# The second GEMM of a spectral mixer: two narrow products become one wide one

## The chip, the cores and the metric

The kernel runs on one core of a Trainium2 chip. The metric is the device time of one execution in microseconds; the lower, the better. The kernel before took 381.93 us, the median of three executions (381.85 to 384.48).

The engines are called as in the profile: PE (matrix products; PEld is its weight load), DVE (vector), ACT (activation), POOL and SP. Here POOL and SP mostly issue transfers in the part of the kernel that is changed.

## The reference

The input is one sequence of S = 2048 tokens with D = 512 channels. Two branches read its normalised form: a 2-D Fourier filter, and a token-mixing MLP with F = 1792 hidden units. The output joins them.

```python
def _B_ref(x, w1, b1, w2, b2):
    h = _layernorm(x, axis=-1)                      # (B, S, D)
    u = jnp.einsum("bsd,sf->bdf", h, w1) + b1       # (B, D, F)
    u = _gelu(u)
    y = jnp.einsum("bdf,fs->bds", u, w2) + b2       # (B, D, S)
    return y.transpose(0, 2, 1)

x = A_x
xn = _layernorm(x, axis=-1)
s = _A_ref(xn, A_w_r, A_w_i)      # irfft2(rfft2(xn) * (w_r + 1j w_i))
g = _silu(_B_ref(xn, B_w1, B_b1, B_w2, B_b2))
return x + s * g
```

All inputs and the output are float32.

## The kernel before

The program has two large parts. The first (up to about 204.7 us) computes the normalisation, the first GEMM (u = gelu(w1 h + b1)) and the forward Fourier transform with its filter. The second, which the change is about, computes the second GEMM, the inverse transform, the gate and the output.

**Precision.** PE is fed with a reduced float32 type. Each float32 operand is split into a high part (a copy by ACT, rounded to that type) and a low part (the difference, by DVE). A product of two operands is then three matmuls: high by high, high by low, low by high. This is the inner loop over `a` at line 940.

**Blocks.** The tokens are laid out as 16 blocks j of 128. The second GEMM works on pairs: pair p takes block j0 = p and block j1 = p + 8, for p = 0 to 7. With the halves of F and the halves of the channels this is a product of 2 x 2 blocks, and it is computed with seven block products instead of eight (a Strassen-like scheme). Each block product is called a form, numbered 1 to 7 and run in the order 1, 2, 5, 6, 3, 7, 4 (`ORDER`). Each form sums over seven tiles of 128 hidden units (`FORMS`), so it is 7 x 3 = 21 matmuls. The operand of w2 for form n is a tile w2f (high part at index 0, low part at index 1), built from loaded blocks a11, a12, a21, s4 and the running sum s1. The operand of u is a tile of 512 columns: 256 high, 256 low (tiles fa, fb, fc, fd; `form_parts` cuts them in two). Those were made once, the last of them (tiles 5 and 6) in the first microseconds of this part.

**PSUM.** Eight banks of 512 float32 columns. In the second GEMM a form uses the first 256 columns of a bank: bx (bank 2 or 3, by the parity of p), by (bank 4), bz (bank 5). Forms 6, 7 and 4 go on summing in the bank of form 1, form 3 in that of form 5. Between them ACT copies a partial sum out: p1 after form 1, v2 after form 6, p5 after form 5 (`copied`, lines 894 to 897). The four output blocks of the pair are c11 = by + p1, c12 = bz + v2, c22 = bx + p5 (DVE adds, `summed`), and c21, which is bx itself after form 4. ACT gates each with a sigmoid-weighted unit (`gate`), DVE multiplies by the filtered branch (`finish`), and a transfer that POOL issues adds it to the output in memory.

**Inverse transform.** Between the forms PE also does four blocks of eight small instructions per pair: `sequence` (line 866) and `channels` (line 875), one of each for j0 and j1. `sequence` writes bank 0 or bank 1, `channels` bank 6 or 7. ACT copies the first's result to a tile yt, which `channels` reads.

**Order.** The engines run their queues in order. In the first part and in the first microseconds of the second, the order is written out by hand (the string `STEPS` and the calls of `rest`, `forms`, `wforms` in lines 815 to 841, with `strict` set). After that the framework's scheduler places the instructions, except those that `keep` holds in program order. `ready` holds w2f tiles made ahead; the pool has three buffers. SP's queue issues the loads of w2 and the gathers yj of the transform's input, in order; POOL's issues the transfers that add the second block to s1 and s4.

**The hand-over (pair 0).** Forms of u for tiles 5 and 6 are still being made when form 1 of pair 0 starts. The sources u of these forms lie in memory (`lstage`) that the last pool `fp` takes over when they are done. The tile p1_0 of the kernel before is allocated in `fp`.

The two lines that cost the matmuls of this part:

```python
for a, (wi, ui) in enumerate(((0, uh), (0, ul), (1, uh))):
    in_turn(j0, T.matmul(o, wf[:, wi, i], ui, start=m + a == 0 and n in (1, 2, 5), stop=m == NH - 1 and a == 2,
```

Of the kernel before, what the change touches and what calls it, by code (L numbers as in the profile page):

```python
# [8 lines left out]
F32 = mybir.dt.float32  # L9
# [109 lines left out]
def spectral_mixer_kernel(tc, x, w1, b1, w2, b2, wk, we, wx, c_f, c_ft, c_d, c_i, c_g, c_h, c_s, out):  # L119
# [11 lines left out]
    def pool(stack, side, name, bufs):  # L131
        return stack.enter_context(tc.tile_pool(name=name, bufs=bufs, side=side, reuse_waits="tile"))
# [9 lines left out]
    with tc.tile_pool(name="ps", bufs=1, space=PSUM) as psp, ExitStack() as left, ExitStack() as right:  # L142
# [222 lines left out]

        def form_parts(n, i):
            t, k = form[i][n]
            return t[:, k, :D // 2], t[:, k, D // 2:]

# [384 lines left out]
        V, A, G, SY = free  # L754
        w2p = pool(right, "right", "w2", 3)
        NP, HD = NJ // 2, D // 2
        ORDER = (1, 2, 5, 6, 3, 7, 4)
# [25 lines left out]
        def w2_forms():  # L783

            for p in range(NP):
                yield w2_form(f"1_{p}", cur["a12"])
                yield w2_form(f"2_{p}", cur["a11"])
                w = w2_form(f"5_{p}", cur["s1"])
                ordered(V.tensor_add(cur["s1"], cur["s1"], cur["a12"]))
                yield w  # L790
                w = w2_form(f"6_{p}", cur["s1"])
                if p == 0:
                    yield w
                if p + 1 < NP:
                    nxt["s1"] = s1_load(p + 1, (w2p, fp)[(p + 1) % 2])
                    nxt["a12"] = w2_load("a12", w2p, p + 1, 1)
                if p:
                    yield w
                V.tensor_add(cur["s1"], cur["s1"], cur["a11"])  # L799
                w = w2_form(f"3_{p}", cur["s1"])  # L800
                if p + 1 < NP:
                    nxt["a11"] = w2_load("a11", w2p, p + 1, 0)
                yield w
                w = w2_form(f"7_{p}", cur["s4"])
                if p + 1 < NP:
                    nxt["s4"] = w2_load("s4", w2p, p + 1, 1, (p + 1 + NP, 1))
                yield w
                w = w2_form(f"4_{p}", cur["a21"])
                if p + 1 < NP:
                    nxt["a21"] = w2_load("a21", fp, p + 1 + NP, 0)  # L810
                    cur.update(nxt)
                yield w
# [4 lines left out]
        strict.append(True)  # L817
        ready = [next(wforms) for _ in range(3)]

        def rest(units, *gelus):  # L820
            for _ in range(units):
                next(streams["h"])
            for _ in gelus:
                next(streams["g"])
        rest(SPLIT, 5)
        rest(4, 12)
        last, last6 = forms(5), forms(6)
        next(last)
        next(last)
        rest(4, 13)  # L830
# [3 lines left out]
        next(last6)  # L834
        next(last6)
        next(last)
        next(last6)
        ready.append(next(wforms))
        run(last)
        run(last6)  # L840
# [3 lines left out]
        HW = [P, HD]  # L844
        made = {"p1_0": fp.tile(HW, F32, name="p1_0", tag="p1")}
        gs = [fp.tile([P, D], F32, name=f"g{j}", tag="g", bufs=3) for j in (0, NP)]
# [16 lines left out]
        def sequence(j, yj):  # L863
            pf = ps[:, j // NP].rearrange("p (b c) -> p b c", c=P)
            for b in range(4):
                in_turn(j, T.matmul(pf[:, b], yj[:, b * P:(b + 1) * P], cft, start=True, stop=True))  # L866
            yt = fp.tile([P, 4, P], F32, name=f"yt{j}", tag="yt", bufs=2)
            A.activation(yt, pf, AF.Copy)
            return yt
# [24 lines left out]
        def copied(name, src):  # L894
            t = made.pop(name, None) or fp.tile([P, HD], F32, name=name, tag=name.split("_")[0])
            A.activation(t, src, AF.Copy)  # L896
            return t

        def gate(g, j, cols, src, scale):
            A.activation(g[:, cols], src, AF.Silu, bias=b2t[:, j:j + 1], scale=scale)  # L900

        def summed(name, a, b):
            t = made.pop(name, None) or fp.tile([P, HD], F32, name=name, tag="c", bufs=2)
            V.tensor_add(t, a, b)  # L904
            return t
# [14 lines left out]
        for p in range(NP):  # L920
# [3 lines left out]
            if p == NP - 1:  # L924
                xr = fp.tile([P, D], F32, name="xr", tag="yj", bufs=3)
                SY.dma_start(xr, x[:, NJ - 1])
            bx, by, bz = ps[:, 2 + p % 2, :HD], ps[:, 4, :HD], ps[:, 5, :HD]
            for k, n in enumerate(ORDER):
# [6 lines left out]
                if k == 5 and p + 1 < NP:  # L935
                    yd = gathered(j1 + 1)
                o = {1: bx, 6: bx, 7: bx, 4: bx, 2: by, 5: bz, 3: bz}[n]
                for m, i in enumerate(FORMS):
                    uh, ul = form_parts(n, i)
                    for a, (wi, ui) in enumerate(((0, uh), (0, ul), (1, uh))):  # L940
                        in_turn(j0, T.matmul(o, wf[:, wi, i], ui, start=m + a == 0 and n in (1, 2, 5), stop=m == NH - 1 and a == 2,  # L941
                                             skip_group_check=n in (6, 3, 7, 4)))
                if n == 1:
# [20 lines left out]
                elif n == 7:  # L964
                    gate(g1, j1, right_, summed(f"c22_{p}", bx, p5), -1.0)
                    if p == 0:
# [6 lines left out]
                else:  # L973
                    gate(g1, j1, left_, bx, -1.0)
                    finish(g1, j1, whole if p + 1 < NP else left_, y1, xr)
# [40 lines left out]
```

## Time and profile before

| | |
|---|---|
| Median of three executions | 381.93 us (381.85 to 384.48) |
| The profiled execution | 382.29 us, of which its span (first to last instruction) is 380.5 us |
| Granted clock of PE | 1.00 throughout |
| Matmuls of the second GEMM, line 941 | 1176 of 256 columns |
| Period of a middle pair | 21.06 us |
| Start of form 1 of pair 0 | 204.70 us |

The profile gives times in us from the start of the span. A row of the groups by line reads: line, engine, operation, output<-input, shapes and count | busy us, mean ns of one | idle time just before, and who ended it. A row of the timeline reads: start, length, engine, line, operation. The length of a matmul or a DVE instruction is longer than its distance to the next one, since they are pipelined; where a rate is needed, the distance of the starts, or the chain of waits, is the better source. L941 is line 941 of the kernel before; lines of the changed kernel are some 1 to 22 higher.

### The profile page before, as it was taken

How to read it: one execution, taken by the hardware profiler on the slowest of the kernel's cores; microseconds unless marked ns; L12 is line 12 of the kernel's file. 1: busy time of each engine (PE TensorE's matmuls, PEld its weight loads, DVE VectorE, ACT ScalarE, POOL GpSimd, SP SyncE). 2: the span in 40 equal slices, each digit the busy share in tenths (PEclk: the TensorE clock that was granted, in tenths of full speed). 3: DMA queues.
4: the chain of work that ended last, by engine and by line, in shares of the span. 5: the costliest groups of instructions: out<-in, count | busy, mean ns of one | idle time of the engine just before them, and what ended most of it. 6: DMA issues, size and time to landing. Idle time of an engine off the chain costs nothing.

```text
span 380.5 us, 7482 instructions
## 1 busy us (share of the span) xinstructions
PE 369.8 (97%) x2760; PEld 327.8 (86%) x2760; DVE 309.0 (81%) x660; ACT 213.3 (56%) x384; POOL 102.3 (27%) x133
## 2 busy tenths in 40 slices
PE   8999999999999999999999799999999999999994
PEld 4888888888877676777779799999999999999994
DVE  5899999865799999999967798776767768777763
ACT  4677755754972365865456765545555555545541
POOL 2133233243511735765400011020303020200100
PEclk9999999999999999999999999999999999999999
DMA  7956467214455767999866599898888888895602
GB/s 249 323 190 231 133 222 239 91 42 128 120 196 179 253 213 258 283 280 307 194 181 155 149 267 188 265 164 263 168 246 184 223 204 193 194 217 158 100 0 56
DMA packets 41945, 73.32 MB, mean 193 GB/s; under 512 B 4180, under 2 KB 25172, under 8 KB 41780
## 3 DMA queue, kind: packets, MB, share of 16 engines
q1 hardware_dynamic: 35460, 58.88, 48.6%
q0 software_dynamic: 6448, 13.96, 21.4%
q8 instruction: 21, 0.34, 0.4%
q14 instruction: 16, 0.13, 0.1%
HBM read 60.24 MB, written 8.13 MB: 180 GB/s over the span
## 4 chain that ended last, share of the span: by engine, by line
PE 86%; DVE 8%; issue 2%; ACT 2%; DMA 1%; SPq 0%; DVEq 0%; ACTq 0%
PE ps L941 34%; PE ps L395 19%; PE ps L678 6%; PE ps L679 5%; PE ps L226 4%; PE ps L687 4%; PE ps L866 4%; PE ps L586 4%; PE ps L875 4%; DVE pq L128 2%; DVE e L128 2%; PE ps L665 1%; PE ps L681 1%; PE ps L600 1%; DMA x<-in_x_dram 1%
## 5 line engine op out<-in xcount | busy, mean ns | idle before, releaser
L395 PE MATMUL ps<-h,w1h 128*128 128x512 f32 x224 | 58.5, 398 | 0.0
L395 PEld LDWEIGHTS ps<-h,w1h 128*128 128x128 f32 x224 | 40.8, 188 | 8.1 <-ACT w1h L387 0.2
L776 DVE TENSOR_TENSOR w2f<-s,w2f 128x896 fp32r<-128x896 f32 x32 | 35.0, 1092 | 14.8 <-ACT w2f L775 13.7
L766 POOL DMA_DIRECT2D s<-in_w_dram x16 | 13.8, 865 | 122.7 <-DMA s<-in_w_dram 35.0
L678 PE MATMUL ps<-h,w1h 128*128 128x512 f32 x112 | 44.9, 401 | 0.0
L679 PE MATMUL ps<-h,w1h 128*128 128x512 f32 x112 | 43.7, 390 | 0.0
L941 PE MATMUL ps<-fb,w2f 128*128 128x256 f32 x336 | 42.9, 282 | 0.6 <-DVE c L904 0.6
L941 PE MATMUL ps<-fa,w2f 128*128 128x256 f32 x336 | 43.4, 283 | 0.0
L941 PE MATMUL ps<-fc,w2f 128*128 128x256 f32 x336 | 41.1, 279 | 2.1 <-ACT p L896 2.1
L941 PEld LDWEIGHTS ps<-fc,w2f 128*128 128x128 f32 x336 | 40.1, 188 | 2.3 <-ACT p L896 2.3
L941 PEld LDWEIGHTS ps<-fb,w2f 128*128 128x128 f32 x336 | 40.6, 188 | 1.4 <-issue 0.8
L941 PEld LDWEIGHTS ps<-fa,w2f 128*128 128x128 f32 x336 | 40.6, 188 | 0.0
L775 ACT ACTIVATE w2f<-s 128x896 fp32r<-128x896 f32 x32 | 30.3, 948 | 16.5 <-DVE s L799 13.5
L776 DVE TENSOR_TENSOR w2f<-a,w2f 128x896 fp32r<-128x896 f32 x24 | 26.1, 1089 | 15.8 <-ACT w2f L775 15.7
L128 POOL TENSOR_TENSOR s<-z,e 128x4 f32<-128x4 f32 x8 | 25.3, 3163 | 37.4 <-DMA z<-e 16.6
L775 ACT ACTIVATE w2f<-a 128x896 fp32r<-128x896 f32 x24 | 22.8, 950 | 21.7 <-PE ps L941 18.2
L395 PE MATMUL ps<-h,w1l 128*128 128x512 f32 x112 | 30.7, 390 | 0.1
L128 ACT ACTIVATE w1h<-w1s 128x512 fp32r<-128x512 f32 (+1 forms) x30 | 17.4, 581 | 22.2 <-PE ps L679 12.9
L678 PEld LDWEIGHTS ps<-h,w1h 128*128 128x128 f32 x112 | 21.0, 188 | 9.0 <-issue 5.0
L687 PE MATMUL ps<-h,w1l 128*128 128x512 f32 x93 | 25.6, 391 | 0.1
L395 PEld LDWEIGHTS ps<-h,w1l 128*128 128x128 f32 x112 | 20.9, 188 | 5.0 <-DVE w1l L390 0.5
L679 PEld LDWEIGHTS ps<-h,w1h 128*128 128x128 f32 x112 | 21.1, 188 | 4.0
(132 smaller groups left out, 730.8 us busy)
## 6 DMA issues: line engine op xcount, KB each, us to landing
a<-in_w_dram SPq DMA_DIRECT2D x24, 448.0 KB
s<-in_w_dram POOLq DMA_DIRECT2D x17, 448.0 KB, 7.0
s<-in_w_dram SPq DMA_DIRECT2D x15, 448.0 KB
w1r<-in_w_dram SPq DMA_DIRECT2D x16, 256.0 KB
z<-e SPq DMA_DIRECT2D x16, 256.0 KB
w1s<-in_w_dram SPq DMA_DIRECT2D x16, 256.0 KB
yj<-ey SPq DMA_DIRECT2D x16, 256.0 KB
x<-in_x_dram SPq DMA_DIRECT2D x15, 256.0 KB
```

Of the source, the lines that this page charges most:

```text
L128: return lambda *a, **k: keep(getattr(engine, name)(*a, **k))
L226: T.matmul(z[:, b], h[:, b * P:(b + 1) * P], c, start=True, stop=True)
L395: T.matmul(ps[:, bank + i], w[wi][:, i * P:(i + 1) * P], hj, start=first and j == 0, stop=last and j == NJ - 1)
L586: keep(T.matmul(pd[:, b * P:(b + 1) * P], ey[:, lo, b].rearrange("p h j -> p (h j)"), cd[:, b], start=True, stop=True))
L678: keep(T.matmul(o, wh[:, sl], hh[j], start=first, stop=False))
L679: keep(T.matmul(o, wh[:, sl], hl[j], start=False, stop=False))
L687: keep(T.matmul(ps[:, bank], wl[:, k * P:k * P + P], hh[j], start=False, stop=final))
L775: ordered(A.activation(wf[:, 0], v, AF.Copy))
L776: ordered(V.tensor_sub(wf[:, 1], v, wf[:, 0].bitcast(F32)))
L866: in_turn(j, T.matmul(pf[:, b], yj[:, b * P:(b + 1) * P], cft, start=True, stop=True))
L875: in_turn(j, T.matmul(pe[:, b % 2, b // 2], yt[:, b], ci[:, b], start=True, stop=True))
L941: in_turn(j0, T.matmul(o, wf[:, wi, i], ui, start=m + a == 0 and n in (1, 2, 5), stop=m == NH - 1 and a == 2, skip_group_check=n in (6, 3, ...
```

## The change

For the pairs 0 to 6 (`both`), the two matmuls with the high part of w2 become one over the whole tile of u, 512 columns, into the whole bank: the high-by-high sums stand in the bank's left half, the high-by-low sums in its right half. The matmul with the low part of w2 adds its 256 columns to the right half. Where a partial sum is read, the right half is now added by one more DVE instruction (`copied`, `summed`). Form 4 gets bank 1 (bw) to itself instead of summing in bx; what bx holds after form 7 is copied out (x22) and goes into c22 and c21. `sequence` uses bank 0 for both blocks. The last pair keeps three matmuls of 256 columns and its banks as before. p1_0 is allocated in the pool of w2's tiles. In the hand-over, w2's form 5 is made after a gelu of tile 5 instead of before, the s1 add later, and the forms of u for tiles 5 and 6 interleave in another order.

```diff
-        def form_parts(n, i):
+        def form_whole(n, i):
             t, k = form[i][n]
-            return t[:, k, :D // 2], t[:, k, D // 2:]
+            return t[:, k]
...
         w2p = pool(right, "right", "w2", 3)
+        p1_0 = w2p.tile([P, D // 2], F32, name="p1_0", tag="p1", bufs=1)
...
-                w = w2_form(f"5_{p}", cur["s1"])
+                yield w2_form(f"5_{p}", cur["s1"])
                 ordered(V.tensor_add(cur["s1"], cur["s1"], cur["a12"]))
-                yield w
+                if p == 0:
+                    yield
...
-        ready = [next(wforms) for _ in range(3)]
+        ready = [next(wforms) for _ in range(2)]
...
         rest(SPLIT, 5)
+        ready.append(next(wforms))
         rest(4, 12)
         last, last6 = forms(5), forms(6)
-        next(last)
-        next(last)
+        for _ in range(3):
+            next(last)
         rest(4, 13)
         rest(4, 6)
         next(last6)
         next(last)
         next(last6)
-        next(last6)
-        next(last)
+        next(wforms)
         next(last6)
         ready.append(next(wforms))
+        next(last6)
         run(last)
         run(last6)
...
-        made = {"p1_0": fp.tile(HW, F32, name="p1_0", tag="p1")}
+        made = {"p1_0": p1_0}
...
-            pf = ps[:, j // NP].rearrange("p (b c) -> p b c", c=P)
+            pf = ps[:, 0].rearrange("p (b c) -> p b c", c=P)
...
         def copied(name, src):
-            t = made.pop(name, None) or fp.tile([P, HD], F32, name=name, tag=name.split("_")[0])
-            A.activation(t, src, AF.Copy)
+            tag = name.split("_")[0]
+            t = made.pop(name, None) or (fp, w2p)[tag == "p1"].tile([P, HD], F32, name=name, tag=tag, bufs=1)
+            A.activation(t, src[:, :HD], AF.Copy)
+            if whole_bank(src):
+                V.tensor_add(t, t, src[:, HD:])
             return t
+
+        def whole_bank(src):
+            return src.shape[-1] == D
...
-            V.tensor_add(t, a, b)
+            V.tensor_add(t, a[:, :HD], b)
+            if whole_bank(a):
+                V.tensor_add(t, t, a[:, HD:])
...
-            bx, by, bz = ps[:, 2 + p % 2, :HD], ps[:, 4, :HD], ps[:, 5, :HD]
+            both = p + 1 < NP
+            bx, by, bz, bw = (ps[:, b] if both else ps[:, b, :HD] for b in (2 + p % 2, 4, 5, 1))
...
-                o = {1: bx, 6: bx, 7: bx, 4: bx, 2: by, 5: bz, 3: bz}[n]
+                o = {1: bx, 6: bx, 7: bx, 4: bw if both else bx, 2: by, 5: bz, 3: bz}[n]
+                opens, joins = n in (1, 2, 5), n in (6, 3, 7) or n == 4 and not both
                 for m, i in enumerate(FORMS):
-                    uh, ul = form_parts(n, i)
-                    for a, (wi, ui) in enumerate(((0, uh), (0, ul), (1, uh))):
-                        in_turn(j0, T.matmul(o, wf[:, wi, i], ui, start=m + a == 0 and n in (1, 2, 5), stop=m == NH - 1 and a == 2,
-                                             skip_group_check=n in (6, 3, 7, 4)))
+                    u, end = form_whole(n, i), m == NH - 1
+                    if both:
+                        in_turn(j0, T.matmul(o, wf[:, 0, i], u, start=m == 0 and not joins, stop=end,
+                                             skip_group_check=True))
+                        in_turn(j0, T.matmul(o[:, HD:], wf[:, 1, i], u[:, :HD], start=False, stop=end,
+                                             skip_group_check=True))
...
                 elif n == 7:
-                    gate(g1, j1, right_, summed(f"c22_{p}", bx, p5), -1.0)
+                    if both:
+                        x22 = copied(f"v2_{p}x", bx)
+                    gate(g1, j1, right_, summed(f"c22_{p}", x22 if both else bx, p5), -1.0)
...
-                    gate(g1, j1, left_, bx, -1.0)
+                    gate(g1, j1, left_, summed(f"c21_{p}", bw, x22) if both else bx, -1.0)
```

More of the change, by code (lines that the diff above doesn't have):

```diff
@@ L936, in spectral_mixer_kernel @@
                     yd = gathered(j1 + 1)
-                o = {1: bx, 6: bx, 7: bx, 4: bx, 2: by, 5: bz, 3: bz}[n]
+                o = {1: bx, 6: bx, 7: bx, 4: bw if both else bx, 2: by, 5: bz, 3: bz}[n]
+                opens, joins = n in (1, 2, 5), n in (6, 3, 7) or n == 4 and not both
                 for m, i in enumerate(FORMS):
-                    uh, ul = form_parts(n, i)
-                    for a, (wi, ui) in enumerate(((0, uh), (0, ul), (1, uh))):
-                        in_turn(j0, T.matmul(o, wf[:, wi, i], ui, start=m + a == 0 and n in (1, 2, 5), stop=m == NH - 1 and a == 2,
-                                             skip_group_check=n in (6, 3, 7, 4)))
+                    u, end = form_whole(n, i), m == NH - 1
[4 more added lines that the diff above has]
+                                             skip_group_check=True))
+                    else:
+                        for a, (wi, ui) in enumerate(((0, u[:, :HD]), (0, u[:, HD:]), (1, u[:, :HD]))):
+                            T.matmul(o, wf[:, wi, i], ui, start=m + a == 0 and opens, stop=end and a == 2,
+                                     skip_group_check=joins)
                 if n == 1:
```

## The prediction

> **What bounds the kernel now.** I read the busy shares first, then one middle pair of the second GEMM by engine, then the chain that ended last, then that pair in order of time.
>
> ```profile
> PE 369.8 (97%) x2760; PEld 327.8 (86%) x2760; DVE 309.0 (81%) x660; ACT 213.3 (56%) x384; POOL 102.3 (27%) x133
> 250.65:271.71 21.06, 21.06 (x183) 20.96 (x181) 15.52 (x31) 10.79 (x19) 3.51 (x4) 1.00 0.87 210
> ```
>
> The second row is the pair p=2: columns after the width 21.06 are busy PE, weight loads, DVE, ACT, POOL, then granted clock, DMA share, GB/s. PE has no free time, DVE 5.5 us, ACT 10.3 us; the clock is at 1.00.
>
> ```profile
> 21.38 4.79 PE ps L395 x21
> ...
> 161.50 0.91 PE ps L687 x4
> ...
> 240.61 0.89 PE ps L875 x8
> 241.50 4.95 PE ps L941 x42
> 246.45 0.89 PE ps L866 x8
> 247.34 2.65 PE ps L941 x21
> 249.99 0.89 PE ps L875 x8
> 250.88 2.48 PE ps L941 x21
> 253.36 0.89 PE ps L866 x8
> 254.25 7.42 PE ps L941 x63
> ...
> 352.67 2.65 PE ps L941 x21
> ```
>
> These are pieces of the chain (start, length). The eight from 240.61 are one whole pair and nothing but PE: seven forms of 21 products and four blocks of inverse transform, 21.06 us together. So the pair costs what its products cost. A product of 256 columns takes 4.95/42 = 117.9 ns; one of 512 columns, in the first GEMM, 4.79/21 = 228.1 ns (0.91/4 = 227.5 in a later stretch). The form at 247.34 (form 4) takes 2.65 instead of 2.48: 0.17 us are a wait.
>
> **Term 1, the wide product.** Per tile of w2 and form, three products of 256 columns become one of 512 and one of 256. The trace has no stream that mixes the widths, so I add the rows: 228.1 + 117.9 = 346.0 instead of 353.6 ns, 7.6 ns saved. Seven pairs (the last keeps the old form) x 7 forms x 7 tiles = 343 times: 2.6 us, all on the path. At one end the wide product saves nothing over two narrow ones (0 us); at the other it takes 227.5 (2.8 us). That it costs more than two narrow ones I exclude, since 228.1 is already less than 235.7 with the same number of columns passed. The middle row is the one with equal tile shapes and type, so 2.6.
>
> [...]
>
> **Term 2, form 4 gets its own bank.** PE around the block before form 4 in pair 3, before and after; fb are the tiles of u, w2f those of w2, yj the transform's input.
>
> ```order
> L941 MATMUL ps<-fb_2503,w2f_3_3402 128x256 x3
> L866 MATMUL ps<-cft,yj_3377 128x128 [waits DMAHW2_49]
> L866 MATMUL ps<-cft,yj_3377 128x128 x3
> L941 MATMUL ps<-fb_1432,w2f_3_3448 128x256 [waits DVE_49,Activation_49]
> L941 MATMUL ps<-fb_1432,w2f_3_3448 128x256 x2
> ```
>
> The same place on PE after the change (L955 is the wide product, L957 the narrow one):
>
> ```order
> L955 MATMUL ps<-fb_2507,w2f_3_3270 128x512
> L957 MATMUL ps<-fb_2507,w2f_3_3270 128x256
> L870 MATMUL ps<-cft,yj_3251 128x128 [waits DMAHW1_49]
> L870 MATMUL ps<-cft,yj_3251 128x128 x3
> L955 MATMUL ps<-fb_1432,w2f_3_3310 128x512 [waits Activation_49]
> L957 MATMUL ps<-fb_1432,w2f_3_3310 128x256 [waits DVE_49]
> ```
>
> The DVE wait of form 4's first product moved to the second, where it is only the low part of w2. The trace shows the old wait:
>
> ```profile
> 256.34 1.09 DVE L799 TENSOR_TENSOR s<-s,a 128x896 f32<-128x896 f32 x1
> ...
> 257.35 0.42 DVE L904 TENSOR_TENSOR c<-ps,p 128x256 f32<-128x256 f32 x1
> ...
> 258.53 1.09 DVE L776 TENSOR_TENSOR w2f<-s,w2f 128x896 fp32r<-128x896 f32 x1 [0.76 <-ACT w2f L775]
> ...
> 262.32 2.72 PE L941 MATMUL ps<-fa,w2f 128*128 128x256 f32 x21
> ...
> 267.79 0.42 DVE L904 TENSOR_TENSOR c<-ps,p 128x256 f32<-128x256 f32 x1
> ...
> 268.35 2.71 PE L941 MATMUL ps<-fb,w2f 128*128 128x256 f32 x21
> ...
> 268.86 0.58 ACT L868 ACTIVATE yt<-ps 128x512 f32<-128x512 f32 x1
> ...
> 270.90 1.05 PE L875 MATMUL ps<-cd,yt 128*128 128x128 f32 x8
> ```
>
> c22 is read out of the shared bank until 268.21, and form 4 starts at 268.35. The 2.65 recurs once in each of the pairs 1 to 6 (247.34 the first, 352.67 the last): 6 x 0.17 = 1.0 us goes, and nothing else is late at that place, since form 4's weights are made a whole form earlier. Pair 7 keeps its wait.
>
> **Term 3, what DVE and ACT get in a pair.** Bank halves have to be joined: one add more after p1, p5, v2, c11, c12, the new copy x22, and two for c21, eight adds; ACT copies x22 and in exchange gates from SBUF. Prices:
>
> ```profile
> L941 PE MATMUL ps<-fb,w2f 128*128 128x256 f32 x336 | 42.9, 282 | 0.6 <-DVE c L904 0.6
> L941 PE MATMUL ps<-fc,w2f 128*128 128x256 f32 x336 | 41.1, 279 | 2.1 <-ACT p L896 2.1
> ...
> L775 ACT ACTIVATE w2f<-s 128x896 fp32r<-128x896 f32 x32 | 30.3, 948 | 16.5 <-DVE s L799 13.5 <-DVE s L789 3.0
> ...
> L904 DVE TENSOR_TENSOR c<-ps,p 128x256 f32<-128x256 f32 x16 | 6.7, 417 | 0.0
> ...
> L896 ACT ACTIVATE p<-ps 128x256 f32<-128x256 f32 x16 | 6.1, 385 | 16.2 <-PE ps L941 14.9 <-DVE fb L296 1.4
> ```
>
> These are groups by line (busy us, mean ns of one, idle before); two DVE steps of the size of an add, in order of time:
>
> ```profile
> 273.45 0.42 DVE L879 TENSOR_TENSOR es<-ps,od 128x256 f32<-128x256 f32 x1
> 273.79 0.41 DVE L880 TENSOR_TENSOR es<-ps,od 128x256 f32<-128x256 f32 x1
> ```
>
> An add lasts 0.42 us, but the next instruction starts 0.34 us after it. So DVE gets 8 x 0.34 to 8 x 0.42 = 2.7 to 3.3 us on top of 15.5, together 18.2 to 18.8 of a pair of 20.5 us (21.06 - 49 x 0.0076 - 0.17). It fits, if no chain runs late. DVE in pair 5 around c11, before (w2fN is the split of w2 for form N, s1 the running sum of w2's blocks, p and c the copies and sums of PSUM):
>
> ```order
> L776 TENSOR_TENSOR w2f6_5_3847<-s1_13_3596,w2f6_5_3847 128x896 [waits PE_49,Activation_49]
> L799 TENSOR_TENSOR s1_13_3596<-s1_13_3596,a11_5_3629 128x896 [waits DVE_49]
> L904 TENSOR_TENSOR c11_5_3876<-ps_58,p1_5_3839 128x256 [waits PE_49]
> L776 TENSOR_TENSOR w2f3_5_3880<-s1_13_3596,w2f3_5_3880 128x896 [waits Activation_49]
> L776 TENSOR_TENSOR w2f7_5_3910<-s4_5_3659,w2f7_5_3910 128x896 [waits DMASW2_49,PE_49,Activation_49]
> ```
>
> And the same stretch of DVE after:
>
> ```order
> L903 TENSOR_TENSOR p1_5_3641<-p1_5_3641,ps_58 128x256 [waits Activation_49]
> L778 TENSOR_TENSOR w2f6_5_3651<-s1_13_3438,w2f6_5_3651 128x896 [waits Activation_49]
> L914 TENSOR_TENSOR c11_5_3673<-ps_58,p1_5_3641 128x256 [waits DVE_49,PE_49]
> L802 TENSOR_TENSOR s1_13_3438<-s1_13_3438,a11_5_3465 128x896 [waits DVE_49]
> L916 TENSOR_TENSOR c11_5_3673<-c11_5_3673,ps_58 128x256 [waits DVE_49]
> L778 TENSOR_TENSOR w2f3_5_3678<-s1_13_3438,w2f3_5_3678 128x896 [waits Activation_49]
> L903 TENSOR_TENSOR p5_5_3699<-p5_5_3699,ps_58 128x256 [waits Activation_49]
> L778 TENSOR_TENSOR w2f7_5_3702<-s4_5_3489,w2f7_5_3702 128x896 [waits DMASW2_49,Activation_49]
> ```
>
> The sum s1 now stands behind c11, so behind the end of form 2: it starts about 257.7 instead of 256.34. Queued behind it are form 3's weights, done at 259.62 today while form 3 starts at 262.32: of 2.7 us of slack 1.35 go, and p5's add, for which form 3 now waits, takes 0.4 more. About 0.95 is left. The other tight chain is ACT's before the block at 270.90: yt is done at 269.44, 1.46 us ahead; the x22 copy (0.39) and the gate of c12 (taken as long, now behind w2's copy) come before it, and 0.7 is left. So I put this term at 0; without the cover each late microsecond costs seven.
>
> **Term 4, the start (pair 0).** The 2.1 us that PE waits on "ACT p" (row above) are one wait, form 6 of pair 0.
>
> ```profile
> 203.45 0.33 SPq L764 DMA_DIRECT2D a<-in_w_dram  x1
> 203.83 1.38 SPq L853 DMA_DIRECT2D yj<-ey  x2
> 204.70 2.63 PE L941 MATMUL ps<-fd,w2f 128*128 128x256 f32 x21
> 205.93 0.42 DVE L296 TENSOR_TENSOR fd<-u,fd 128x256 fp32r<-128x256 f32 x1 [1.60 <-ACT fd L295]
> 208.70 0.42 DVE L315 TENSOR_TENSOR u<-u 128x256 f32<-128x256 f32 x1
> ...
> 210.08 0.43 DVE L318 SCALAR_TENSOR_TENSOR u<-u 128x256 f32<-128x256 f32 x1
> 210.42 1.29 DVE L296 TENSOR_TENSOR fc<-u,fc 128x512 fp32r<-128x512 f32 x2
> 212.63 1.28 DVE L296 TENSOR_TENSOR fb<-u,fb 128x512 fp32r<-128x512 f32 x2
> 213.84 1.08 DVE L799 TENSOR_TENSOR s<-s,a 128x896 f32<-128x896 f32 x1
> 214.39 2.65 PE L941 MATMUL ps<-fc,w2f 128*128 128x256 f32 x21 [2.11 <-ACT p L896]
> ```
>
> p1_0 lay in memory that fb's sources held; now it has its own tile, and the wait goes. But DVE is reordered. DVE's rows behind the u steps of tile 6, before (fa to fd are the forms of u, with the tile's number):
>
> ```order
> L296 TENSOR_TENSOR fc5_2500<-u5_2438,fc5_2500 128x2x256 [waits PE_49,Activation_49]
> L296 TENSOR_TENSOR fc6_2504<-u6_2470,fc6_2504 128x2x256 [waits PE_49,Activation_49]
> L776 TENSOR_TENSOR w2f6_0_2507<-s1_8_2406,w2f6_0_2507 128x896 [waits Activation_49]
> L296 TENSOR_TENSOR fb5_2499<-u5_2438,fb5_2499 128x2x256 [waits Activation_49]
> L296 TENSOR_TENSOR fb6_2503<-u6_2470,fb6_2503 128x2x256 [waits Activation_49]
> L799 TENSOR_TENSOR s1_8_2406<-s1_8_2406,a11_0_2411 128x896 [waits DVE_49]
> ```
>
> And DVE after, from the s1 add that stood far ahead of them:
>
> ```order
> L791 TENSOR_TENSOR s1_8_2407<-s1_8_2407,a12_0_2410 128x896
> L315 TENSOR_TENSOR u6_2474<-u6_2474 128x256 [waits DVE_49]
> L903 TENSOR_TENSOR p1_0_2406<-p1_0_2406,ps_58 128x256 [waits Activation_49]
> L316 TENSOR_TENSOR u6_2474<-u6_2474 128x256 [waits DVE_49]
> L317 SCALAR_TENSOR_TENSOR u6_2474<-u6_2474 128x256 [waits DVE_49]
> L318 SCALAR_TENSOR_TENSOR u6_2474<-u6_2474 128x256 [waits DVE_49]
> L778 TENSOR_TENSOR w2f6_0_2504<-s1_8_2407,w2f6_0_2504 128x896 [waits Activation_49]
> L296 TENSOR_TENSOR fc6_2508<-u6_2474,fc6_2508 128x2x256 [waits Activation_49]
> ```
>
> fc6's low part now comes behind the s1 add, p1's add and w2f6. From 205.93: fd 0.42, fc5 and fa6 0.65 each, s1 1.08, four u steps 1.8, p1 0.42, w2f6 1.08, fc6 0.65, less overlaps of 0.07: done at 212.3 or so. Form 5 wants it at 204.70 + 2 x 2.42 + 6/7 x 2.42 = 211.6 (2.42 is a form of seven 346 ns): a new wait of 0.75. Form 6 then starts at 212.7, 1.7 earlier, 0.15 of it term 1. Form 3's weights: s1 behind fb (1.28) and its own 1.08, done 214.7; ACT 0.95 beside three adds of DVE; low part 1.09: 216.9, while PE wants it at 212.7 + 2.42 + 0.89 + 0.23 = 216.2. So 0.65 is lost again. Net 1.7 - 0.15 - 0.65 = 0.9 us. Ends: 2.1 (no new wait) and -1.1 (rival C).
>
> **Sum.** 2.6 + 1.0 + 0 + 0.9 = 4.5 us. The profiled execution took 382.29 us, 1.8 outside its span: 377.8. It lies 0.36 above the median of 381.93, so 377.4 as a median.
>
> **Rivals.** B, the wide product saves nothing, because the fixed part of a product is set by its neighbour's weight load and not by the count: 382.3 - 1.9 = 380.4, by the median 380.0. For it: weight loads are busy 20.96 of 21.06 us; against it: wide products in a row already run at 7.6 ns less. [...]
>
> C, pair 0 loses more than it gains. The load of a12 waits for the s1 add, now done at 208.7, and the two yj gathers and a21 stand behind it on SP: they leave 5.3 us later.
>
> ```profile
> s<-in_w_dram POOLq DMA_DIRECT2D x17, 448.0 KB, 7.0
> ```
>
> If a gather takes 8 us from 209.1, the block after form 6, wanted at 215.1, waits 2.0: term 4 is -1.1 and the median 382.29 - 2.5 - 0.36 = 379.4. Against it: the queue is nearly empty then.
>
> D, slower: DVE becomes the bound at form 3.
>
> ```profile
> DVE w2f L776 <- ACT w2f L775: 29.4, 31, 3.2
> ```
>
> This row of the waits (us in total, times, longest) gives 29.4/8 = 3.7 us per pair. If each add costs 0.46 (the spacing of the four dependent DVE steps from 208.70 to 210.08) a pair is 15.5 + 3.7 = 19.2 us of DVE, and if its waits on ACT stay, since form 3's chain goes DVE, ACT, DVE, 22.9: 7 x 1.8 = 12.9 us more, 0.9 less at the start, median 394. It decides once form 3's chain is over 0.95 us later than worked out. Against it: the 0.34 us spacing.
>
> [...]
>
> **Numbers.** A measurement here can tell 1% from no change, 378.1 and 385.7. Forecast 0.60, B 0.12, C 0.15, D 0.13. Of the forecast's 0.60 I put 0.06 above 378.1, from its terms' ends: faster 0.54, same 0.33, slower 0.13. The range takes the terms' better ends, 2.8 + 1.0 + 2.1 = 5.9, down to 376.0, and B and C, up to B with no gain at the start (382.3 - 1.0 - 0.36 = 380.9); D lies outside.
>
> **What would show it.** Right: a middle pair of 20.5 us, form 4 without 0.17, wide and narrow product together 346 ns, DVE 18 to 19 us busy in a pair, no PE wait on "ACT p" and a short one on DVE's fc in pair 0. Wrong: PE idle before forms 3 or 7 with DVE named (D), a pair of 20.9 (B), PE idle on yj (C).

## The result, and the profile after

The changed kernel took 380.22 us, median of 22 runs, against 382.19 of the kernel before beside it: a ratio of 0.9935, 95% interval 0.9917 to 0.9954. By the ratio that is about 2.5 us less, by the medians 2.0. Predicted were 377.4, that is 4.5 us less. Executions of 385.25, 701.53 (the first profiled one) and 741.61 us, and in the experiments one of 2081.4 and one of 383.92, were disturbed and are left out of the ratios. The profile shown is that of a repeat execution of the same kernel (380.25 us, span 378.5; before: 382.29, span 380.5). Busy shares first, from the page of the changed kernel:

```profile
PE 368.9 (97%) x2417; PEld 311.6 (82%) x2417; DVE 327.9 (87%) x716; ACT 214.5 (57%) x391; POOL 102.2 (27%) x133
```

PE has 343 products fewer and only 0.9 us less to do; DVE has 56 instructions more, 18.9 us. Next the second GEMM in stretches, from form 1 of a pair to form 1 of the next (each cut 0.24 us ahead of the form's start): the changed kernel's pairs 0 to 3. The columns after the width are busy PE, weight loads, DVE, ACT, POOL, then clock, DMA share, GB/s.

```profile
204.26:227.90 23.64, 23.05 (x146) 20.20 (x145) 20.90 (x46) 15.21 (x26) 2.57 (x3) 1.00 0.69 189
227.90:249.50 21.60, 21.09 (x133) 18.61 (x132) 18.04 (x39) 11.74 (x20) 3.26 (x4) 1.00 0.88 233
249.50:270.32 20.82, 20.82 (x133) 18.62 (x132) 18.43 (x39) 10.46 (x20) 4.19 (x6) 1.00 0.92 219
270.32:291.17 20.85, 20.85 (x133) 18.64 (x132) 18.35 (x39) 10.93 (x20) 3.43 (x5) 1.00 0.91 217
```

The same stretches, pairs 0 and 1, of the kernel before:

```profile
204.46:229.33 24.87, 22.76 (x195) 22.50 (x194) 19.49 (x41) 15.45 (x26) 2.57 (x3) 1.00 0.80 214
229.33:250.40 21.07, 21.07 (x182) 20.97 (x181) 15.47 (x30) 10.80 (x19) 4.37 (x5) 1.00 0.87 212
```

Three things stand here. Pair 0 gained 1.23 us. Pair 1 lost 0.53. The pairs after it take 20.83 us instead of 21.06, a gain of 0.23 where 0.54 was predicted, and PE is busy in all of it: nothing waits in them, so the products themselves are slower than worked out. The chain of waits of the changed kernel lists its wide products; these are from forms 2, 5 and 6 of pair 2 (start, length):

```profile
255.09 0.23 PE ps L955
255.44 0.24 PE ps L955
255.80 0.24 PE ps L955
...
260.04 0.24 PE ps L955
```

From 255.09 to 260.04 are 14 steps: 353.6 ns for a wide and a narrow product together, exactly what three narrow ones took before (3 x 117.9), and not 346.0. On average over a middle pair it is (20.83 - 4 x 0.89)/49 = 352.4 ns, and in the first forms of pair 0 a little less. PE in order of time: form 2, two products of form 5 (its first and its last tile's) and the first of form 6:

```profile
206.95 0.39 PE L955 MATMUL ps<-fa,w2f 128*128 128x512 f32 x1
207.18 0.28 PE L957 MATMUL ps<-fa,w2f 128*128 128x256 f32 x1
207.30 0.40 PE L955 MATMUL ps<-fa,w2f 128*128 128x512 f32 x1
...
209.39 0.40 PE L955 MATMUL ps<-fc,w2f 128*128 128x512 f32 x1
...
212.13 0.50 PE L955 MATMUL ps<-fc,w2f 128*128 128x512 f32 x1 [0.48 <-DVE fc L296]
...
212.59 0.40 PE L955 MATMUL ps<-fc,w2f 128*128 128x512 f32 x1
```

Seven steps in 2.44 us are 348.6 ns each. The row of 212.13 is the wait of form 5 on DVE's fc. The profile counts 0.48 us of idle time, with ends of matmuls that are modelled; by the starts form 5 takes 3.20 us (209.39 to 212.59) instead of 2.44, so the wait costs 0.76, and 0.75 was predicted. The loss in pair 1 is a wait of PE. One of the waits of PE from 204 to 253 us, and one of ACT from 228 to 253 us (us in total, times, longest):

```profile
PE ps L879 <- ACT yt L872: 0.5, 1, 0.5
```

```profile
ACT w2f L777 <- DMA a<-in_w_dram: 4.2, 2, 3.8
```

ACT stands 3.8 us at the split of a12 for pair 2, whose transfer has not landed; yt comes behind it on ACT, and the block that PE wants next comes behind yt.

### The profile page after: what moved, and what is told of

It is laid out like the page before. It is cut to its first block, busy times and chain, and to the rows that moved or that the text cites. A ratio compares the mean times of both kernels' runs of the same rounds, so it can differ in the third digit from the quotient of the medians.

```text
span 699.8 us, 6864 instructions
## 1 busy us (share of the span) xinstructions
PE 693.5 (99%) x2417; PEld 507.3 (72%) x2417; DVE 334.2 (48%) x716; ACT 217.4 (31%) x391; POOL 77.8 (11%) x133
## 4 chain that ended last, share of the span: by engine, by line
PE 99%; DVE 0%; POOL 0%; ACT 0%; issue 0%; POOLq 0%
PE ps L396 22%; PE ps L955 20%; PE ps L957 10%; PE ps L679 8%; PE ps L680 7%; PE ps L688 6%; PE ps L587 4%; PE ps L226 4%; PE ps L961 4%; PE ps L870 4%; PE ps L879 4%; PE ps L666 1%; PE ps L682 1%; PE ps L601 1%; PE ps L385 1%; ACT g L910 0%
## 5 line engine op out<-in xcount | busy, mean ns | idle before, releaser
L396 PE MATMUL ps<-h,w1h 128*128 128x512 f32 x224 | 114.8, 687 | 0.0
L396 PEld LDWEIGHTS ps<-h,w1h 128*128 128x128 f32 x224 | 66.8, 307 | 31.8 <-issue 28.9
L679 PE MATMUL ps<-h,w1h 128*128 128x512 f32 x112 | 76.4, 682 | 0.0
L680 PE MATMUL ps<-h,w1h 128*128 128x512 f32 x112 | 75.4, 673 | 0.0
L955 PE MATMUL ps<-fa,w2f 128*128 128x512 f32 x98 | 60.1, 628 | 0.0
L396 PE MATMUL ps<-h,w1l 128*128 128x512 f32 x112 | 59.0, 673 | 0.0
L955 PE MATMUL ps<-fc,w2f 128*128 128x512 f32 x98 | 58.8, 615 | 0.0
L955 PE MATMUL ps<-fb,w2f 128*128 128x512 f32 x98 | 58.7, 612 | 0.0
L236 DVE TENSOR_TENSOR o<-zt 128x256 f32<-128x256 f32 x16 | 6.8, 426 | 101.5 <-ACT zt L231 101.5
L679 PEld LDWEIGHTS ps<-h,w1h 128*128 128x128 f32 x112 | 33.7, 301 | 26.0 <-issue 24.3
L688 PE MATMUL ps<-h,w1l 128*128 128x512 f32 x93 | 49.0, 673 | 0.0
L231 ACT ACTIVATE zt<-ps 128x512 f32<-128x512 f32 x16 | 9.6, 598 | 122.6 <-PE ps L226 122.6
L396 PEld LDWEIGHTS ps<-h,w1l 128*128 128x128 f32 x112 | 33.1, 295 | 19.0 <-issue 16.7
L680 PEld LDWEIGHTS ps<-h,w1h 128*128 128x128 f32 x112 | 33.3, 297 | 15.7 <-issue 14.2
L128 DVE TENSOR_TENSOR w1l<-w1s,w1h 128x384 fp32r<-128x384 f32 (+1 forms) x25 | 15.2, 612 | 57.9 <-ACT w1h L128 25.4
L688 PEld LDWEIGHTS ps<-h,w1l 128*128 128x128 f32 x93 | 28.2, 303 | 15.4 <-issue 13.9
```

The lines of the kernel that those rows point to most:

```text
L128: return lambda *a, **k: keep(getattr(engine, name)(*a, **k))
L396: T.matmul(ps[:, bank + i], w[wi][:, i * P:(i + 1) * P], hj, start=first and j == 0, stop=last and j == NJ - 1)
L679: keep(T.matmul(o, wh[:, sl], hh[j], start=first, stop=False))
L680: keep(T.matmul(o, wh[:, sl], hl[j], start=False, stop=False))
L688: keep(T.matmul(ps[:, bank], wl[:, k * P:k * P + P], hh[j], start=False, stop=final))
L955: in_turn(j0, T.matmul(o, wf[:, 0, i], u, start=m == 0 and not joins, stop=end, skip_group_check=True))
```

## The experiments

**The changed kernel again** (no edit).

> The changed kernel as it is, for a profile whose PE runs at the full rate. The theory of the prediction: a middle pair of 20.5 us, wide and narrow product together 346 ns, no wait ahead of form 4, and in pair 0 a wait of 0.7 us on DVE's fc in place of the 2.1 us on ACT's p1. Rival B (the wide product saves nothing): a pair of 20.9 us. Rival D (DVE late at form 3): PE idle before form 3 or 7 with DVE named. The measured gain of about 2.4 us is half of the 4.5 us forecast, so at least one term has to be short by about 2 us; if it is the start, pair 1 begins no earlier than 229 us.

It took 380.1 us, median, against 382.0: 0.9936, 0.9912 to 0.9959. Its profile is the one above. The form 4 wait is gone and DVE is 18.4 us busy in a pair, as expected; the pair of 20.5 us isn't there, and neither is an idle PE ahead of forms 3 or 7 in pairs 2 to 6. Pair 1 begins at 228.14 us, not at 229 or later, so the start isn't the term that is short by about 2 us. What remains is to find which term failed, and why.

**Form 4's own bank alone**, on the kernel before.

```diff
-            pf = ps[:, j // NP].rearrange("p (b c) -> p b c", c=P)
+            pf = ps[:, 0].rearrange("p (b c) -> p b c", c=P)
...
-            bx, by, bz = ps[:, 2 + p % 2, :HD], ps[:, 4, :HD], ps[:, 5, :HD]
+            both = p + 1 < NP
+            bx, by, bz, bw = (ps[:, b, :HD] for b in (2 + p % 2, 4, 5, 1))
...
-                o = {1: bx, 6: bx, 7: bx, 4: bx, 2: by, 5: bz, 3: bz}[n]
+                o = {1: bx, 6: bx, 7: bx, 4: bw if both else bx, 2: by, 5: bz, 3: bz}[n]
...
+                    if both:
+                        x22 = copied(f"v2_{p}x", bx)
...
-                    gate(g1, j1, left_, bx, -1.0)
+                    gate(g1, j1, left_, summed(f"c21_{p}", bw, x22) if both else bx, -1.0)
```

> The kernel before with one part of the change: form 4 of pairs 0 to 6 goes to a bank of its own, x22 is copied by ACT and both halves are joined by DVE from the copy; all products keep their 256 columns and pair 0 its old order. Term 2 says that the 0.17 us ahead of form 4 go in six pairs: 1.0 us less than before, a middle pair of 20.89 instead of 21.06. Rival: the added copy and add delay yt, the block after form 4 waits for it, and nothing is gained.

Pairs 1 and 2 of this kernel:

```profile
230.99:251.87 20.88, 20.88 (x182) 20.88 (x181) 15.86 (x32) 11.15 (x20) 4.29 (x5) 1.00 0.86 210
251.87:272.76 20.89, 20.89 (x182) 20.89 (x181) 15.85 (x32) 11.19 (x20) 3.48 (x4) 1.00 0.91 215
```

0.17 to 0.18 us less than 21.06, six times: term 2 is right, and PE is busy throughout, so the rival's late yt didn't come. The whole: 0.9969, 0.9943 to 0.9994. Its executions fall into two groups, six at 380.8 to 381.1 us and five at 382.6 to 383.4, those of the kernel before too (11 of 23 at 381.8 to 382.2, 12 at 383.8 to 384.5); between the lower groups the bank is worth 1.0 us. What divides the groups is shown with p1_0 below.

**p1_0 apart, alone**, on the kernel before.

```diff
+        p1_0 = w2p.tile([P, D // 2], F32, name="p1_0", tag="p1", bufs=1)
...
-        made = {"p1_0": fp.tile(HW, F32, name="p1_0", tag="p1")}
+        made = {"p1_0": p1_0}
...
```

> The kernel before with one part of the change: p1_0 has its own tile beside w2's splits; products, banks and the order in which pair 0's splits are made stay. The 2.1 us wait of PE on ACT's p1 should go, and since DVE's fc and fb of the last tile are not pushed back here, little should take its place: form 6 about 1.5 to 2.1 us earlier and the whole 1.5 to 2.1 us shorter than before. Rival: form 3's split of w2, which comes behind fb, becomes late and takes half of it back: 1.0 us.

Pair 0, and PE's only waits from 204 to 260 us:

```profile
204.10:228.22 24.12, 23.24 (x195) 22.78 (x194) 19.39 (x41) 14.96 (x26) 2.60 (x3) 1.00 0.78 195
```

```profile
PE ps L943 <- DVE w2f L777: 0.9, 2, 0.6
```

The wait of 2.1 us on p1 is gone, and pair 0 is 0.75 us shorter, not 1.5 to 2.1: two waits for w2's splits from DVE, in forms 6 (0.25) and 3 (0.63), take its place. The rival was right. The ratio is 0.995, 0.993 to 0.9971, and all twelve executions lie between 380.85 and 381.93; the group at 384 is gone.

**Wide products first**, on the changed kernel.

```diff
-                for m, i in enumerate(FORMS):
+                tiles = list(enumerate(FORMS))
+                for part, (m, i) in [(s, t) for s in (0, 1) for t in tiles] if both and p else [(s, t) for t in tiles for s in (0, 1)]:
                     u, end = form_whole(n, i), m == NH - 1
-                    if both:
+                    if both and part == 0:
                         in_turn(j0, T.matmul(o, wf[:, 0, i], u, start=m == 0 and not joins, stop=end,
                                              skip_group_check=True))
+                    elif both:
                         in_turn(j0, T.matmul(o[:, HD:], wf[:, 1, i], u[:, :HD], start=False, stop=end,
                                              skip_group_check=True))
...
```

> The changed kernel with another order of products in pairs 1 to 6: in every form the seven wide products first, then the seven narrow ones; nothing else differs. In the changed kernel a wide and a narrow product take 351 to 353 ns together in these pairs. Theory L (a wide product runs at 227 ns, but behind a narrow one, which gives the next weight load only 118 ns, it starts late): six wide in a row at 227, one mixed, 345 a triple, a pair shorter by 0.35 us and the whole by 2.1 us. Theory R (in this stage the columns go by at about 0.46 ns each whatever the width, against 0.443 in the first GEMM): wide 233 to 235, narrow 118, no difference within 0.3 us.

377.82 us, 0.9873, 0.9833 to 0.9912. Pair 2, and pieces of the chain in it (start, length; L956 is the wide product, L959 the narrow one):

```profile
248.54:269.02 20.48, 20.48 (x133) 18.40 (x132) 18.25 (x39) 11.04 (x20) 3.90 (x5) 1.00 0.89 213
```

```profile
250.65 0.80 PE ps L959 x7
...
252.34 1.62 PE ps L956 x7
253.96 0.79 PE ps L959 x7
254.75 1.60 PE ps L956 x7
256.35 0.82 PE ps L959 x7
```

The same products in another order: 1.60/7 = 229 to 1.62/7 = 231 ns for a wide one, 0.79/7 = 113 to 0.82/7 = 117 for a narrow one, 344 to 346 for the two together in the forms shown, and the pair of 20.5 us that the prediction had. Theory L's times came, and theory R (a rate of the stage) falls. L's reason, the weight load, is another matter. The starts in pairs 2 to 6 of the changed kernel are 120 ns apart on average from a narrow product to the wide one behind it, 3 to 7 more than among narrow ones, and 233 from a wide to the narrow one behind it, 2 to 4 more than among wide ones. L has the whole loss in the first of these steps.

**Groups of two tiles**, on the version with the wide products first.

```diff
-                for part, (m, i) in [(s, t) for s in (0, 1) for t in tiles] if both and p else [(s, t) for t in tiles for s in (0, 1)]:
+                for part, (m, i) in [(s, t) for k2 in range(0, NH, 2) for s in (0, 1) for t in tiles[k2:k2 + 2]] if both and p else [(s, t) for t in tiles for s in (0, 1)]:
```

> The changed kernel with the products of pairs 1 to 6 in groups of two tiles: two wide, two narrow, and so on; between the changed kernel (a wide behind a narrow product seven times in a form) and the one with all seven wide products first (at most once). If the loss belongs to each wide product that stands behind a narrow one, a form has four of them here, and a pair lies half way between 20.83 and 20.48: 20.66. If the loss belongs to the load of the stage or to its mean width, which are the same in all three, there is no reason for half way: 20.8, or 20.5 as soon as two wide ones meet.

```profile
249.91:270.56 20.65, 20.65 (x133) 18.50 (x132) 18.43 (x39) 10.46 (x20) 3.94 (x5) 1.00 0.96 222
```

Pair 2 takes 20.65 us, half way as expected (378.91 us in two executions, 0.9887, 0.9837 to 0.9936). So the loss goes with the number of changes between narrow and wide: (20.83 - 20.48)/(7 x 6) = 8 ns for each of the six that the grouping takes out of a form. That is all that term 1 had hoped to save per triple.

**All products wide**, on the changed kernel.

```diff
-                        in_turn(j0, T.matmul(o[:, HD:], wf[:, 1, i], u[:, :HD], start=False, stop=end,
+                        in_turn(j0, T.matmul(o, wf[:, 1, i], u, start=False, stop=end,
```

> The changed kernel with the narrow products made wide in pairs 0 to 6: low part of w2 times high and low part of u, so all products of these pairs have 512 columns (it computes one small term more than needed). Theory L: with no narrow product every weight load has a whole wide product beside it, 227 ns each: a form 3.18 us, a pair 25.8. Theory R: 0.46 ns a column, 235 each: a form 3.30, a pair 26.6.

It took 414.69 us in its only execution. Pair 2, and some products of form 2 and 5 in pair 2 in order of time:

```profile
257.90:283.95 26.05, 26.05 (x133) 21.99 (x132) 18.86 (x39) 11.17 (x20) 3.48 (x4) 1.00 0.70 165
```

```profile
264.62 0.39 PE L955 MATMUL ps<-fa,w2f 128*128 128x512 f32 x1
264.85 0.39 PE L957 MATMUL ps<-fa,w2f 128*128 128x512 f32 x1
...
265.54 0.39 PE L955 MATMUL ps<-fc,w2f 128*128 128x512 f32 x1
265.77 0.39 PE L957 MATMUL ps<-fc,w2f 128*128 128x512 f32 x1
```

Four steps from 264.62 to 265.54, 230 ns each, so L's side (227), not R's (235); the 26.05 us lie 0.25 above L and 0.55 below R. Wide products in a row do run at nearly the first GEMM's pace in this stage (230 against 228.1 ns). It is the mixture that costs: 353.6 ns for a wide and a narrow product.

**Wide first in pair 0's later forms too**, on the version with the wide products first.

```diff
-                for part, (m, i) in [(s, t) for s in (0, 1) for t in tiles] if both and p else [(s, t) for t in tiles for s in (0, 1)]:
+                for part, (m, i) in [(s, t) for s in (0, 1) for t in tiles] if both and (p or joins or n == 4) else [(s, t) for t in tiles for s in (0, 1)]:
```

> The version with the wide products first, now also in forms 6, 3, 7 and 4 of pair 0. Four forms at 0.05 to 0.07 us less each, and form 3 of pair 0 wants the low part of its weights 1.6 us later, so that its wait of about 0.45 us there goes: 0.4 to 0.7 us less than with pairs 1 to 6 alone, about 377.2 where that took 377.7.

377.99 us (0.9859, 0.983 to 0.9888), no less than without it: a miss. Pair 0 took 23.68 us, against 23.64. The wait of form 3 on DVE (0.4 us on PE's weight load, with pairs 1 to 6 alone) is gone, but two waits for yt have come:

```profile
PE ps L879 <- ACT yt L872: 0.6, 2, 0.4
PE ps L956 <- DVE fc L296: 0.5, 1, 0.5
```

One of them is ahead of the block after form 3 in pair 0. With DVE out of the way yt on ACT is late there; the other is the wait in pair 1.

**p1_0 back in the forms' memory**, on the version with the wide products first.

```diff
-        p1_0 = w2p.tile([P, D // 2], F32, name="p1_0", tag="p1", bufs=1)
...
-        made = {"p1_0": p1_0}
+        made = {"p1_0": fp.tile(HW, F32, name="p1_0", tag="p1")}
...
```

> The version with the wide products first in pairs 1 to 6, but p1_0 again in memory that is free only when the last forms of u are made, as before the change. Term 4: PE waits about 2 us on ACT's p1 again ahead of form 6 of pair 0, form 3's wait of 0.45 goes with it, so 1.2 to 1.7 us longer than with p1_0 apart (378.9 to 379.4). The granted clock fell to 0.5 for 3.4 us behind this wait in the profiled execution with form 4's own bank alone, and about half of the executions of the kernel before and of that one lie 2.3 us above the others, of the one with p1_0 apart none of twelve. If the wait is the cause, such executions come back here, at 381 to 382.

Two executions took 378.73 and 378.99 us, five 380.4 to 381.3; with p1_0 apart four of six lay at 377.3 to 377.9, so p1_0 is worth about 1.2 us. The upper group is back, and the profiled execution is one of it. A PE wait of pair 0, and the stretch behind it:

```profile
PE ps L955 <- DVE p L902: 1.9, 1, 1.9
```

```profile
215.33:218.73 3.40, 3.40 (x11) 2.94 (x12) 2.96 (x5) 3.16 (x4) 0.00 (x0) 0.53 0.79 249
```

The mean granted clock over 3.40 us is 0.53, and only 11 products are done in it. Form 4's bank alone had the same in its profiled execution, and the kernel before, with the same wait of 2.1 us, not in its own; first the one, then the other:

```profile
214.16:217.57 3.41, 3.10 (x14) 3.10 (x15) 2.26 (x3) 3.04 (x5) 0.85 (x1) 0.54 0.44 61
```

```profile
214.16:217.57 3.41, 3.18 (x28) 3.19 (x29) 2.19 (x3) 3.04 (x5) 0.86 (x1) 1.00 0.39 54
```

So the wait of about 2 us has a second price that is due in some executions only: half clock for 3.4 us behind it. With that stretch pair 0 of form 4's bank alone took 26.45 us, against 24.87 in the kernel before without it: 1.6 us, most of the 1.9 between the two groups of that kernel. The granted clock of each execution divides the groups too: of 74 executions of the kernel before, beside the experiments, the 33 of the upper group have a mean of 0.994 to 0.996, the other 41 of 0.997 to 1.000. So the stretch makes the upper group, and p1_0 apart takes it away.

**The old order of pair 0's splits**, on the changed kernel.

```diff
-                yield w2_form(f"5_{p}", cur["s1"])
+                w = w2_form(f"5_{p}", cur["s1"])
                 ordered(V.tensor_add(cur["s1"], cur["s1"], cur["a12"]))
-                if p == 0:
-                    yield
+                yield w
...
-        ready = [next(wforms) for _ in range(2)]
+        ready = [next(wforms) for _ in range(3)]
...
```

> The changed kernel, but the start of the second GEMM in its old order: form 5's split is yielded after the sum s1, the last forms of u and the split for form 6 as before; p1_0 stays apart. Term 4 blames the new order for a wait of form 5 on fc of the last tile (0.65 us measured) and half a microsecond ahead of form 3. With the old order fc of the last tile is in time, but, as with p1_0 apart in the kernel before, form 6 waits some 0.5 and form 3 some 0.9 us: 0.3 us longer than the changed kernel. If only the wait of form 5 goes and nothing takes its place, it is 0.6 shorter.

380.56 us (0.9938, 0.9915 to 0.9961), 0.4 more than the changed kernel's 380.1, within the two intervals. PE's waits from 204 to 253 us:

```profile
PE ps L955 <- DVE w2f L778: 0.8, 2, 0.6
PE ps L877 <- ACT yt L870: 0.6, 1, 0.6
```

Pair 0 takes 24.28 us, 0.64 more than with the new order: fc is in time, and the splits for forms 6 and 3 are late instead. The first expectation held in kind; the new order is a small gain, not the cost that the prediction feared.

**Fewer transfers**, on the changed kernel, and beside it **the changed kernel** and **the version with the wide products first** as they were.

```diff
-            return w2_load("s1", where, p + NP, 0, (p + NP, 1), queue)
+            return w2_load("s1", where, p + NP, 0, None if p == 2 else (p + NP, 1), queue)
...
-                    nxt["s4"] = w2_load("s4", w2p, p + 1, 1, (p + 1 + NP, 1))
+                    nxt["s4"] = w2_load("s4", w2p, p + 1, 1, None if p == 1 else (p + 1 + NP, 1))
```

> The changed kernel without two transfers: the adding loads of the second halves of s1 and s4 for pair 2 (0.45 MB each) are left out, so that pair's blocks of w2 are incomplete sums; all instructions on the engines stay. The trace of the changed kernel has the DMA engines 0.97 busy from 221 to 245 us, ACT waiting 3.8 us for a12 of pair 2, and behind that a PE wait of 0.8 us for yt in pair 1 (21.60 instead of 20.83 us). If the full DMA engines are the cause, a12 comes a microsecond or more earlier, PE does not wait for yt and pair 1 takes 20.8 us: up to 0.8 us less than the changed kernel beside it. If it is the order on ACT alone, pair 1 stays at 21.4 to 21.7.

> The changed kernel as it is, on the same chip as the version with the wide products first and the one with fewer loads, so that they can be set against each other: about 379.4 to 380.5, 2.0 to 2.4 below the undisturbed runs of the kernel before.

> The version with the wide products first in pairs 1 to 6, word for word as before, beside the changed kernel on one chip: a pair of 20.48 against 20.83, six pairs: 2.1 us less than the changed kernel; 377.3 to 378. If the earlier difference came from the chip, less than 1 us.

Fewer transfers: 379.85 us, five executions within 379.3 to 380.3. Its pair 1:

```profile
228.15:249.00 20.85, 20.85 (x133) 18.64 (x132) 18.46 (x39) 10.92 (x20) 2.20 (x3) 1.00 0.87 225
```

No wait is left in pair 1, nor one of ACT for a transfer. Beside it the changed kernel took 380.15 us (0.9945, 0.9918 to 0.9971): eight of twelve executions 379.5 to 380.4, four 382.0 to 383.5. Its profiled execution is one of the four; pair 1, and ACT's longest wait in it:

```profile
228.91:251.93 23.02, 21.58 (x133) 18.68 (x132) 18.00 (x39) 11.03 (x20) 3.72 (x5) 1.00 0.86 213
```

```profile
ACT w2f L777 <- DMA s<-in_w_dram: 5.4, 1, 5.4
```

2.2 us are lost behind another late block of w2, s1 this time; PE waits ahead of forms 6 and 3, on DVE's p and w2f and not on yt. The version with the wide products first took 378.77 us (0.9897, 0.9869 to 0.9926), 1.4 less than the changed kernel beside it in the median and 2.05 less in the lowest, where 2.1 less and 377.3 to 378 were expected; the median is a miss. Its profiled execution (382.31 us) has the worst case of pair 1, on PE in order of time, and the clock behind it:

```profile
251.09 2.07 PE L879 MATMUL ps<-cd,yt 128*128 128x128 f32 x8 [3.29 <-ACT yt L872]
```

```profile
250.81:254.22 3.41, 3.13 (x11) 2.87 (x12) 2.71 (x6) 1.85 (x4) 1.76 (x3) 0.54 0.86 163
```

So pair 1 waits in some executions and not in others. Pair 1 took 20.48, 21.10, 21.26, 21.60, 21.66, 23.02 and 24.87 us in the profiled executions of the kernels with p1_0 apart and both widths, where 20.5 to 20.8 is a pair without a wait. The kernel before, form 4's bank alone, p1_0 apart alone and p1_0 back show no such wait. That isn't because they hold PE up longer in pair 0: the old order has the wait, and its pair 0 is as long as that of p1_0 apart alone (24.28 and 24.12 us). The share of the DMA engines from 221 to 245 us, in the changed kernel's first profile:

```profile
221.00:245.00 24.00, 24.00 (x154) 21.54 (x153) 21.02 (x53) 11.17 (x21) 3.55 (x5) 1.00 0.97 241
```

It is 0.92 with fewer transfers. But it is 0.92 also in the execution of the changed kernel that lost 2.2 us, and 0.98 in the first profile with the wide products first, which lost nothing. So the share of the DMA engines doesn't tell the cases apart. ACT's wait for a block of w2 does. First the wide products first in their first profile, where nothing was lost; then the same kernel where pair 1 took 24.87 us:

```profile
ACT w2f L777 <- DMA a<-in_w_dram: 2.9, 1, 2.9
```

```profile
ACT w2f L777 <- DMA a<-in_w_dram: 6.5, 1, 6.5
```

Waits of 3.1 to 3.9 us cost PE 0.6 to 0.8 us, the one of 5.4 us 2.2. That late blocks of w2 cost the time is read off these profiles; why they are late is open. The version with fewer transfers has one profile, and its time is not clearly below the lower executions of the changed kernel.

## Why the prediction was right in its range and wrong in its sum

The difference of the two spans, 2.0 us, splits by the stretches above: 0.2 already before the second GEMM (scatter: the profiles start it between 204.3 and 205.3 us), 1.23 in pair 0, 0.53 lost in pair 1, 0.23 in each of pairs 2 to 6 (1.1), nothing in pair 7.

**Term 1** (2.6 us) failed. Of 0.23 us a pair, 0.17 to 0.18 are the bank (form 4's bank alone shows them by themselves), so the wide product brings 0.05 a pair instead of 0.37; with some 0.1 more in the 348.6 ns triples of pair 0, about 0.4 us. The step that failed is "I add the rows: 228.1 + 117.9 = 346.0". Both rows came from streams of one width, the first GEMM and the second, and "the trace has no stream that mixes the widths" was rightly said and then not priced: the lower end of that term, 0, was the nearer one. The wide first order shows that the sum holds as soon as equal widths stand together (344 to 346 ns). A reason that fits, but that no run shows, is that a weight load doesn't get shorter with the product beside it: the loads of pair 2 are recorded at 0.19 us each, before wide and narrow products alike. In the blocks of 128 columns, 8 products follow at 0.89/8 = 111 ns, though at the pace of the wide ones (228/512 = 0.445 ns a column) 128 columns would take 57 by my estimate; if the load sets the 111, there is hardly room for it behind a narrow product of 113. But the runs separate only the order. Part of the loss, 2 to 4 ns a triple, lies in the step from wide to narrow, and with each change of width the columns written in the bank change as well; which of the three, load, width or columns, is at fault stays open.

**Term 2** (1.0 us) was right in place and size: 1.0 us between the lower groups, 0.17 to 0.18 a pair.

**Term 3** (0) was right for DVE and wrong for pair 1. DVE is 18.4 us busy in a pair (18.2 to 18.8 predicted), and no pair from 2 to 6 waits ahead of form 3. The other tight chain, yt on ACT ahead of the block after form 4, was put at 0.7 us of slack. It broke in pair 1, and not by the copies and gates of that sum but by a late transfer that holds up ACT in front of yt: 0.8 us in the first profile, 4.4 in the worst, the half clock behind the wait included. In a third the late block cost 2.2 us by way of DVE, ahead of forms 6 and 3.

**Term 4** (0.9 us) came out at about 1.1 (1.23 less the 0.1 of the wide products). The removed wait and the new ones are all there, by the starts: 2.26 us ahead of form 6 are gone (form 5 took 4.74 from 209.65 to 214.39 instead of 2.48), 0.76 on fc have come as predicted, and about 0.4 for form 3's split instead of 0.65. That removing p1's wait alone is worth 0.75 us and not 2.1 was right in kind. Not foreseen is its second gain, the stretches of half clock behind that wait: 33 of those 74 executions of the kernel before took 383.4 to 385.0 us, none of the twelve with p1_0 apart alone. This gain lies in the ratio, but not in the prediction, which went by one profile that had no such stretch.

**Rivals.** B is nearly what happened to the wide product, and its sign, a pair of 20.9 us, came (20.83). That its sum, 380.0, is within 0.2 of the measured 380.22 is in part luck: the 0.8 us lost in pair 1, which B's sum didn't have, make up for what the wide product, the start and the scatter ahead of it brought beyond B. Its reason, the neighbour's weight load, fits and isn't shown. A chance of 0.12 was too low: the row against it, wide products in a row, didn't speak of a mixture. C's mechanism, late transfers, came one pair later than said, on w2's blocks and not on the gathers. D didn't come: DVE is 2.4 us short of being the bound, and the 56 adds cost 18.9/56 = 0.34 us each.

## What to carry to other kernels

The duration of a product in a row of its own kind wasn't its duration between others here: by the rows a wide and a narrow one come to 346.0 ns, in the mixture they took 353.6. When a change that mixes widths is priced by adding such rows, the lower end is the safe one, and putting equal widths together (here seven wide, then seven narrow, no product changed: 20.48 instead of 20.83 us a pair) can be worth as much as the change. A wait of some 2 us on PE cost more than its length here, in some executions only (pair 0 took 26.45 us with half clock behind the wait in form 4's bank alone, 24.87 in the kernel before without it), so the times of several executions belong beside the one profile. When a wait at the start is taken away, look for new waits in the next stretch, and in more than one profile: pair 1 lost 0 to 4.4 us here, in executions of one and the same kernel.

## What the runs showed that was not expected

The pace of a product went with its neighbours: a 512-column product took 227 to 228 ns in the first GEMM, 229 to 231 among its like in the second, and with the narrow one behind it the two took 353.6 ns instead of 344 to 346. In these three orders the cost went with the number of changes (20.83, 20.65, 20.48 us a pair with seven, four and one group in a form).

The granted clock fell to half behind waits of PE in three profiled executions: a mean of 0.53 over 3.40 us behind 1.9 us (p1_0 back), of 0.54 over 3.41 us behind 2.1 us (form 4's bank alone) and behind 3.3 us (the wide products first, beside the changed kernel). Behind an equal wait of 2.1 us in the kernel before it stayed at 1.00. What divides these cases the runs don't show.
